# Ten heads through float32 transposes on TensorE, GpSimd copies for q and k, and new prices for the DMA queue

## The chip, the cores and the metric

One core of one Trainium2 chip runs the program. The metric is the device time of one execution in microseconds (us). Of the kernel before, three runs gave 1230.02 us (median), 1227.51 and 1231.83; a difference of about 0.3% is what such a comparison can tell from none.

Engines: PE (TensorE, matmuls; PEld is its weight load), DVE (VectorE), ACT (ScalarE), POOL (GpSimd), SP (SyncE, whose queue issues all DMA transfers here). Each engine works through its own list of instructions in order, and waits on semaphores for the others.

## The reference

Attention with a block mask over 8 batches of 8 heads (64 heads), 576 positions, 64 columns, then a mixer:

```python
scores = scale * q @ k.T                       # per head: 576 x 576
scores = where(block_i >= block_j, scores, -1e9)     # blocks of 64 positions
attn = exp(scores - max); attn = attn / (sum(attn) + 1e-9)
x = concat over heads of (attn @ v)            # 8 x 576 x 512, float32
u = x + (xt @ U @ V) transposed                # U: 576 x 32, V: 32 x 576, xt: x with positions last
out = u + relu(u @ w_ch1) @ w_ch2              # w_ch1: 512 x 2048, w_ch2: 2048 x 512
```

Everything is float32. The weights and U, V come from the host as float64 words, and the kernel turns them to float32 on the chip.

## The kernel before

**Attention.** A head's 576 query rows are cut into five tiles, i = 0 to 4 (tile 0 of 64 rows, the others of 128); tile i sees 128 i + 64 keys, so its scores are 128 x (128 i + 64). `split_qk` fetches q and k, transposed by the host, into `raw`. Heads 0 to 11 (`FS = 12`) multiply `raw` in float32 (L961). Later heads split q and k in a high and a low part (`q2`, `k1` by ACT; `q1`, `k2` by POOL, L908 and L909) and run two passes (L965, L966); for that the high part also has to lie in partitions 64 to 127, where two DMA transfers put it (L911, L912).

`softmax` puts the scores in PSUM: tile 4 in the one pair of banks `bw`, tile 3 in a bank of its own, tile 2 in another, tiles 1 and 0 in a third. DVE finds the row maximum (L979), ACT the exponential with its sum, in place in PSUM (L989). `normalise` takes the reciprocal of the sum (L1007, L1010); ACT writes the scaled probabilities as float16 (`nat`, L1022), DVE what is left of them as a second float16 (L1027), after which the bank is free. A DMA transpose (L1033) turns `nat` into `tr`, with keys in the partitions. Tiles 3 and 4 form group 1 and tiles 0 to 2 group 0, one transpose each. `split_v` cuts v into three bfloat16 pieces (POOL, L926 and L930). `apply_v` multiplies the pieces with `tr` in 33 matmuls a head (L1056); ACT and DVE join the two halves of the result (L1060, L1063) in `xt`. After two heads, `mix` transposes `xt` on PE (L1082), applies U and V (L1096, L1111) and adds (L1116).

**The mixer.** The hidden width of 2048 is worked in two halves. For the first, 16 chunks of 288 positions go through `ffn_chunk`: 96 matmuls for w1 (L477), ReLU by ACT into `hh` with the low part `hl` by DVE, 96 matmuls for w2 (L500), all of 288 columns. The first two chunks are cut in two turns. This fills PE while attention runs. The second half is done behind that by `block_products` (L671, 2688 matmuls), with fewer products by sums of blocks. Weight tiles are fetched 512 KB at a time and converted by ACT, DVE and POOL (`split64`, L327).

**What sets the order.** Nothing is issued as it is written. Each step is handed to `Plan.add` with its engine, a price in ns, a priority and the buffers that it reads and writes. `Plan.issue` (L176) plays the steps against these prices: whenever an engine is free, it takes the ready step of the lowest priority number, attention by head number, and the FFN's PE work behind all of attention (`F = 1e6 + ...`). PSUM banks are handed out there too, from lists of free ones. What comes out is one fixed list of instructions for each engine; on the chip the lists don't change. So a price moves no work by itself, it only changes the lists. Of the FFN's 3072 matmuls of the first half, these lists put 252 ahead of the end of head 16 and 2256 ahead of the end of head 63 (the last).

Of the kernel before, what the change touches and what calls it, by code (L numbers as in the profile page):

```python
# [18 lines left out]
P = 128  # L19
# [29 lines left out]
UP = 2.0 ** 15  # L49


TAIL = {"PE": 165, "DVE": 78, "ACT": 105, "POOL": 20, "SP": 0}
# [7 lines left out]
WH = 2  # L60
XB, XT, XL = 700.0, 15.6, 2500

LEAST = 2.0 ** -15
MOST = 2.0 ** 16 * (2.0 - 2.0 ** -3 - 2.0 ** -23)

QS = (0, 320, S)

TILES = ((1, 2, 0), (3, 4))
# [61 lines left out]
class Rest:  # L130
# [11 lines left out]
    def append(self, x):  # L142
        self.pool.append(x)


# [120 lines left out]
def attention_then_mixer(  # L266
# [27 lines left out]
    psp = ctx.enter_context(tc.tile_pool(name="psp", bufs=1, space=bass.MemoryType.PSUM))  # L294
    actx, pctx = ExitStack(), ExitStack()
    ap = actx.enter_context(tc.tile_pool(name="ap", bufs=1))
    hp = ctx.enter_context(tc.tile_pool(name="hp", bufs=1, side="right"))

# [134 lines left out]
    ul_r = ring(fp, KC, [P, T], F32R, "ul")  # L433
    hh_t, hl_t = (hp.tile([P, FC + 2, T], F32R, name=x) for x in ("hh", "hl"))
    hh_r, hl_r = ([Buf(t[:, n, :]) for n in range(FC + 2)] for t in (hh_t, hl_t))
    ot_t = fp.tile([P, 3, T], F32, name="ot")
    ot_r = [Buf(ot_t[:, n, :]) for n in range(3)]

    ph_t, pl_t = ([Buf(t[:, 2 * n : 2 * n + 2, :]) for n in range(FC // 2 + 1)] for t in (hh_t, hl_t))

    ffn_done = [Buf() for _ in range(NCHUNK)]

    def ffn_chunk(c, w, wb, fr=range(FC), turn=0):
# [5 lines left out]
        for k in range(KC):  # L449
            if b > 0 or turn:  # L450
                add(
                    "SP", 630, E, lambda k=k: nc.sync.dma_start(out=ur[k].ap, in_=u_d[b][:, k, o : o + T]),
                    u_s[b][k].parts, [ur[k]], after=DL,
                )
        for k in range(KC):
            uh, ul = uh_r[k], ul_r[k]
            add("ACT", _act(T, True), E, lambda u=ur[k], h=uh: nc.scalar.copy(h.ap, u.ap), [ur[k]], [uh])
            add(
                "POOL", 780, E, lambda u=ur[k], h=uh, l=ul: nc.gpsimd.tensor_sub(l.ap, u.ap, f32(h.ap)),  # L459
                [ur[k], uh], [ul],  # L460
            )
            if turn:
                add(
                    "SP", 630, E, lambda k=k: nc.sync.dma_start(out=ur[k].ap, in_=o_d[b][:, k, o : o + T]),
                    [o_s[c][k]], [ur[k]], after=DL,
                )
# [24 lines left out]
        for m in range(KC):  # L491
            ps = Buf(pool=banks)
            ms = slice(m * P, (m + 1) * P)
            ops = [(wn, f, x) for f in fr for wn, x in (("w2h", 0), ("w2l", 0), ("w2h", 1))]
            for g in range(0, len(ops), GM):

                def products(g=g, ps=ps, ms=ms, ops=ops):
                    for i in range(g, g + GM):
                        wn, f, x = ops[i]
                        nc.tensor.matmul(ps[:, :T], w()[wn][:, f, ms], hs[f][x].ap, start=(i == 0), stop=(i == len(ops) - 1))  # L500
# [9 lines left out]
            add(  # L510
                "SP", 630, E, lambda ot=ot, m=m: nc.sync.dma_start(out=o_d[b][:, m, o : o + T], in_=ot.ap), [ot],
                [o_s[c][m]], after=DL,
            )

    def block_products():
# [164 lines left out]
        for b in range(B):  # L680
# [8 lines left out]
            for t in range(CPB):  # L689
                o = t * T  # L690
                for k in range(2):
                    add(
                        "SP", 630, E,
                        lambda t=t, k=k, o=o, b=b, ur_at=ur_at: nc.sync.dma_start(
                            out=ur_at(t, k), in_=u_d[b][:, 2 * k : 2 * k + 2, o : o + T]
                        ),
                        [x for m in (2 * k, 2 * k + 1) for x in u_s[b][m].parts], [ur[t][k]], after=DL,
                    )
                for i in range(2):
                    add(  # L700
                        "SP", 630, E,
                        lambda t=t, i=i, o=o, b=b: nc.sync.dma_start(
                            out=acc_at(t, i), in_=o_d[b][:, 2 * i : 2 * i + 2, o : o + T]
                        ),
                        o_s[b * CPB + t][2 * i : 2 * i + 2], [acc[t][i]], after=DL,
                    )
# [39 lines left out]
            for stage, (parts, (w, _)) in enumerate(zip(blocks(src, STAGES2), STAGES2)):  # L746
# [8 lines left out]
                if last:  # L755

                    for i, bank in enumerate(banks):
# [8 lines left out]
                        add(  # L766
                            "SP", 630, E,
                            lambda i=i, o=b * S: nc.sync.dma_start(out=out[:, 2 + i, o : o + T], in_=acc_at(0, 1)[:, i, :]),
# [13 lines left out]
                for t, i in {3: ((0, 0),), 4: ((1, 0),), 5: ((1, 1),), 6: ((0, 1),)}.get(stage, ()):  # L782
                    o = b * S + t * T
                    add(
                        "SP", 630, E,
                        lambda t=t, i=i, o=o: nc.sync.dma_start(out=out[:, 2 * i : 2 * i + 2, o : o + T], in_=acc_at(t, i)),
# [5 lines left out]
    make_identity(nc, ident.ap)  # L792

    warm = buf(ap, [P, 1], F32, "warm")
    nc.vector.memset(warm.ap, 0.0)
# [8 lines left out]
    ss_r = [b.split(5) for b in ring(ap, 2, [P, 5], F32, "ss")]  # L804

    nat_r = [[b.split(len(TILES[g])) for b in ring(ap, 1, [P, NB[g] * P], F16, f"nat{g}")] for g in range(2)]
    tr_r = [ring(ap, 2, [P, NB[g], P], F16, f"tr{g}") for g in range(2)]
# [30 lines left out]
    for j in range(2):  # L838
        nc.vector.memset(ss_r[j].ap, 1.0)
    for g in range(2):  # L840
        for r in nat_r[g]:
            nc.vector.memset(r.ap, 0.0)

# [33 lines left out]
    def split_qk(h, pr):  # L877
# [9 lines left out]
        if h in (FS - 2, FS - 1):  # L887

            for n, (x, o) in enumerate(((q2, 0), (k2, S))):
# [3 lines left out]
                )  # L893
        add("SP", 820, pr, fetch, writes=[raw], after=DL)
        if h < FS:
# [14 lines left out]

        add("SP", 600, pr, lambda: nc.sync.dma_start(out=f32(q1[64:P]), in_=f32(q2[top])), [q2], [q1], after=DL)  # L911
        add("SP", 600, pr, lambda: nc.sync.dma_start(out=f32(k1[64:P]), in_=f32(k1[top])), [k1], [k1], after=DL)  # L912

    def split_v(h, pr):
        s = h % 2
        raw, v2 = vr_r[h // 2 % 2], v2_r[s]
        if s == 0:
            add(
                "SP", 910, pr,
                lambda: nc.sync.dma_start(out=raw[:, :, 0:64], in_=v[h // 2].rearrange("p s j d -> p (s j) d")),  # L920
                writes=raw.parts, after=DL,
            )
        mine, part = raw[:, 5 * s : 5 * s + 5, :], raw.parts[s]
        high = mine.bitcast(BF16)
# [11 lines left out]
    def softmax(h, tiles, pr):  # L936
# [48 lines left out]
        for i, at in parts:  # L985
            rows = P if i else 64

            def exponentials(i=i, at=at, rows=rows):
                nc.scalar.activation(  # L989
                    view(i, at), view(i, at), AF.Exp, bias=mx[:rows, i : i + 1], accum_out=ss[:rows, i : i + 1],  # L990
                )

            exps[i] = (bank, lambda i=i, at=at: view(i, at), Buf(), wide)
            add(
# [4 lines left out]
    def normalise(h, g, pr):  # L999
# [11 lines left out]

        add("DVE", 180, pr, inverse, [ss.parts[i] for i in tiles], [rv.parts[i] for i in tiles])
        for i in sorted(tiles, reverse=True):
# [20 lines left out]
        )  # L1034

    def apply_v(h, g, pr):
        s = h % 2
# [4 lines left out]
        me = slice(64 * s, 64 * s + 64)  # L1042
        vr, v2, tmp, tr = vr_r[h // 2 % 2], v2_r[s], take(tmp_r, "tmp"), tr_r[g][s]
        high = vr.ap.bitcast(BF16)
# [24 lines left out]
    def mix(p, pr):  # L1069
# [34 lines left out]
        for c in range(CPB):  # L1104
# [14 lines left out]
            if b == 0:  # L1119
                add(  # L1120
                    "SP", 630, pr, lambda sums=sums, dst=dst: nc.sync.dma_start(out=dst, in_=sums), [to],
                    [u_s[b][m].parts[c]], after=DL,
                )
        if b > 0:
            add(
                "SP", 820, pr, lambda: nc.sync.dma_start(out=u_d[b][:, m, :], in_=ut.ap), ut.parts, u_s[b][m].parts,
                after=DL,
# [9 lines left out]
    for h in range(NH):  # L1137
        pr = 1000.0 * h
        if h + 1 < NH:
            split_qk(h + 1, max(pr - LA, 1.0))  # L1140
        for g, tiles in ((1, (4, 3)), (0, (2, 1, 0))):
# [3 lines left out]
        for g in (1, 0):  # L1145
            apply_v(h, g, pr + 30)
        if h + 1 < NH:
# [3 lines left out]
        if h == min(WH, NH - 1):  # L1151
# [3 lines left out]
            load_w1(lambda: wa, 0, wab, lambda n: WP2 + WP3 * n, (1,), [gate])  # L1155
            load_w2(lambda: wa, 0, wab, lambda n: WP4 + WP3 * (n - FH), [gate], ks=range(FH, FC))

    for n in range(2):
# [44 lines left out]
```

## Time and profile before

| | |
|---|---|
| median of three runs | 1230.02 us |
| the profiled execution | 1232.24 us, span of its instructions 1230.5 us |
| PE busy | 1130.9 us, 92% |
| DVE, ACT, POOL busy | 998.9 us (81%), 802.0 us (65%), 324.8 us (26%) |
| mean granted clock of PE | 0.971 |
| DMA queue q1, share of 16 engines | 67.6% over the span |

Busy time of PE is that of overlapping matmuls. A row of groups reads: line, engine, operation, out<-in, shape, count, then busy us and mean ns of one, then idle time of the engine ahead of them and what ended it. A row of waits reads: who waited, for whom, us in total, times, longest. A row of the timeline reads: start and length in us, engine, line, operation, operands, count of merged instructions. A row of transfers reads: out<-in, queue, operation, count, KB each, median us from issue to landing.

### The profile page before, as it was taken

How to read it: one execution, taken by the hardware profiler on the slowest of the kernel's cores; microseconds unless marked ns; L12 is line 12 of the kernel's file. 1: busy time of each engine (PE TensorE's matmuls, PEld its weight loads, DVE VectorE, ACT ScalarE, POOL GpSimd, SP SyncE). 2: the span in 40 equal slices, each digit the busy share in tenths (PEclk: the TensorE clock that was granted, in tenths of full speed). 3: DMA queues.
4: the chain of work that ended last, by engine and by line, in shares of the span. 5: the costliest groups of instructions: out<-in, count | busy, mean ns of one | idle time of the engine just before them, and what ended most of it. 6: DMA issues, size and time to landing. Idle time of an engine off the chain costs nothing. (4 is left out here: it accounts for less than half of the span.)

```text
span 1230.5 us, 25276 instructions
## 1 busy us (share of the span) xinstructions
PE 1130.9 (92%) x9170; PEld 1067.1 (87%) x9170; DVE 998.9 (81%) x2058; ACT 802.0 (65%) x1944; POOL 324.8 (26%) x336
## 2 busy tenths in 40 slices
PE   6766895899989998998998989999999999999998
PEld 5545784888988888988898889999999999999998
DVE  7899877777787787787778875686998899889887
ACT  6777786688978778798878874343554444444543
POOL 3223454443434353353434431111000000000000
PEclk8788997999999999999999999999999999999999
DMA  8998899999999989989999994533330330330221
GB/s 152 206 211 184 195 209 195 207 200 202 192 192 185 202 185 190 193 172 217 172 211 180 188 190 94 176 112 108 97 100 27 107 116 25 92 116 31 87 78 39
DMA packets 362603, 185.62 MB, mean 151 GB/s; under 512 B 299760, under 2 KB 343792, under 8 KB 362480
## 3 DMA queue, kind: packets, MB, share of 16 engines
q1 hardware_dynamic: 362480, 184.03, 67.6%
q8 instruction: 72, 1.18, 0.4%
q14 instruction: 51, 0.42, 0.1%
HBM read 76.23 MB, written 29.49 MB: 86 GB/s over the span
## 5 line engine op out<-in xcount | busy, mean ns | idle before, releaser
L1056 PE MATMUL ba<-tr,vr 128*128 128x64 f16 (+2 forms) x1408 | 159.9, 235 | 29.5 <-DVE nat L1027 8.4
L671 PE MATMUL bb<-hh,w1l 128*128 128x288 f32 x704 | 170.1, 295 | 0.0
L671 PE MATMUL bb<-hh,w1h 128*128 128x288 f32 x704 | 169.4, 295 | 0.0
L1056 PEld LDWEIGHTS <-vr 128*128 128x128 bf16 x1408 | 103.0, 102 | 51.3 <-issue 19.7
L500 PE MATMUL bf<-hh,w2h 128*128 128x288 f32 x432 | 134.7, 312 | 1.3 <-DVE ot L506 1.3
L1027 DVE SCALAR_TENSOR_TENSOR nat<-ba,rv,nat 128x448 f16<-128x448 f32 (+3 forms) x248 | 110.0, 470 | 24.7 <-ACT nat L1022 22.5
L500 PE MATMUL bf<-hl,w2h 128*128 128x288 f32 x432 | 128.5, 297 | 0.0
L500 PE MATMUL bf<-hh,w2l 128*128 128x288 f32 x432 | 128.1, 297 | 0.0
L989 ACT ACTIVATE ba<-ba,mx 128x448 f32<-128x448 f32 (+3 forms) x248 | 108.1, 436 | 25.8 <-DVE mx L979 22.5
L671 PE MATMUL bb<-hl,w1h 128*128 128x288 f32 x576 | 123.0, 295 | 0.1
L671 PEld LDWEIGHTS bb<-hh,w1l 128*128 128x128 f32 x704 | 122.9, 190 | 0.0
L671 PEld LDWEIGHTS bb<-hh,w1h 128*128 128x128 f32 x704 | 121.9, 188 | 0.0
L1056 PE MATMUL ba<-tr,vv 128*128 128x64 f16 (+2 forms) x704 | 119.7, 234 | 0.0
L1022 ACT ACTIVATE nat<-ba,rv 128x448 f16<-128x448 f32 (+3 forms) x248 | 103.6, 462 | 14.4 <-DVE rv L1010 13.0
L625 ACT CAST hh<-hb 128x576 fp32r<-128x576 f32 x98 | 65.9, 672 | 60.6 <-PE bb L671 59.4
L908 POOL TENSOR_TENSOR q<-raw,q 64x576 fp32r<-64x576 f32 x52 | 74.6, 1435 | 93.6 <-ACT q L902 90.0
L979 DVE TENSOR_REDUCE mx<-ba 128x1 f32<-128x448 f32 (+3 forms) x248 | 92.0, 403 | 4.2 <-PE ba L966 3.2
L671 PEld LDWEIGHTS bb<-hl,w1h 128*128 128x128 f32 x576 | 91.9, 188 | 0.4 <-DVE hl L626 0.4
L477 PE MATMUL bf<-uh,w1l 128*128 128x288 f32 x456 | 90.5, 301 | 0.0
L459 POOL TENSOR_TENSOR ul<-ur,uh 128x288 fp32r<-128x288 f32 x72 | 59.7, 854 | 115.9 <-PE bg L477 68.9
L477 PE MATMUL bf<-uh,w1h 128*128 128x288 f32 x456 | 82.5, 303 | 7.6 <-DVE hl L485 6.7
L909 POOL TENSOR_TENSOR k<-raw,k 64x576 fp32r<-64x576 f32 x52 | 74.0, 1422 | 45.6 <-ACT k L907 34.5
(162 smaller groups left out, 3134.6 us busy)
## 6 DMA issues: line engine op xcount, KB each, us to landing
raw<-in_qk_dram SPq DMA_DIRECT2D x63, 288.0 KB, 4.2
st<-in_w_dram SPq DMA_DIRECT2D x32, 512.0 KB, 4.4
o_d<-ot SPq DMA_DIRECT2D x72, 144.0 KB, 2.4
vr<-in_v_dram SPq DMA_DIRECT2D x32, 320.0 KB, 4.9
ur<-u_d SPq DMA_DIRECT2D x64, 144.0 KB, 2.9
whole<-o_d SPq DMA_DIRECT2D x32, 288.0 KB, 3.1
out_dram<-whole SPq DMA_DIRECT2D x31, 288.0 KB, 2.2
ur<-u_d SPq DMA_DIRECT2D x30, 288.0 KB, 3.6
```

Of the source, the lines that this page charges most:

```text
L459: "POOL", 780, E, lambda u=ur[k], h=uh, l=ul: nc.gpsimd.tensor_sub(l.ap, u.ap, f32(h.ap)),
L477: nc.tensor.matmul(ps[:, :T], w()[wn][:, k, fs], m[k].ap, start=(i == 0), stop=(i == len(ops) - 1))
L500: nc.tensor.matmul(ps[:, :T], w()[wn][:, f, ms], hs[f][x].ap, start=(i == 0), stop=(i == len(ops) - 1))
L625: add("ACT", _act(2 * T, True), E, lambda: nc.scalar.copy(h.ap, x[0]()), [x[1]], [h])
L671: nc.tensor.matmul(bank[:, i, :T], x()[:, w(k)], p.ap[:, k, :], start=first and n == 0, stop=last and n == len(ops) - 1)
L908: add("POOL", 1380, pr, lambda: nc.gpsimd.tensor_sub(q1[top], raw[top, 0:S], f32(q2[top])), [raw, q2], [q1])
L909: add("POOL", 1380, pr, lambda: nc.gpsimd.tensor_sub(k2[top], raw[top, S : 2 * S], f32(k1[top])), [raw, k1], [k2])
L979: lambda i=i, at=at: nc.vector.tensor_reduce(out=mx[: P if i else 64, i : i + 1], in_=view(i, at), op=ALU.max, axis=AX.XY if wide else AX. ...
L989: nc.scalar.activation(view(i, at), view(i, at), AF.Exp, bias=mx[:rows, i : i + 1], accum_out=ss[:rows, i : i + 1],)
L1022: lambda x=x, hi=hi, rows=rows, i=i: nc.scalar.activation(hi, x(), AF.Copy, scale=rv[:rows, i : i + 1]),
L1027: lambda x=x, hi=hi, lo=lo, rows=rows, i=i: nc.vector.scalar_tensor_tensor(out=lo, in0=x(), scalar=rv[:rows, i : i + 1], in1=hi, op0=ALU.m ...
L1056: nc.tensor.matmul(o, w, r, start=(i == 0), stop=(i == len(ops) - 1))
```

## The change

1. **Heads 0 to 9** (`FP = 10`). The exponential goes to float32 tiles in SBUF (`pt_r`, one buffer each for tiles 0 to 3 and two for tile 4). POOL scales them in place. `transpose` turns the blocks of 128 x 128 on PE in float32 (15 a head, with `swap`, an identity whose halves are exchanged, where a half block goes to the other partitions); ACT, and DVE for one of four blocks, copy them to `pw_r`. `apply_v` is then one float32 product per key block, 8 a head of 1600 columns together, and its result is copied once. These heads have no `nat`, no DMA transpose, no `split_v`. Their tiles lie where the FFN's `hh` and `hl` come later (`hidden`), so the FFN's first ReLU comes behind head 9.
2. **Scores of later heads** take the groups (4), (3, 0) and (2, 1): two single banks and tile 4's pair.
3. **Tile 4** may take a pair of its own or, when both halves are free and more than two single banks are, the last two single banks (`Wide`).
4. **q and k**: POOL copies the high parts to partitions 64 to 127 instead of two DMA transfers a head (heads 12 to 63).
5. **Prices of the DMA queue** (SP) in the plan: 630 becomes 440, 820 becomes 560, a transpose `XB + XT * 8 * NB` goes from 2198 and 2946 ns to 1500 and 2700.

```diff
+FP = 10
+PB = (1, 1, 1, 1, 2)
-XB, XT, XL = 700.0, 15.6, 2500
+XB, XT, XL = -900.0, 25.0, 2300
+class Wide:
+    def __bool__(self):
+        return bool(self.own) or (
+            len(self.singles) > 2 and all(any(x is y for y in self.singles) for x in self.halves)
+        )
+    def pop(self, _):
+        if self.own:
+            return self.own.pop()
+        for x in self.halves:
+            del self.singles[next(n for n, y in enumerate(self.singles) if y is x)]
+        return self.pair
...
-    banks_a = [psa.tile([P, 512], F32, name=f"ba{i}") for i in range(6 - FB)]
-    banks_w = [psa.tile([P, 2, 512], F32, name="bw")]
+    pairs_a = [psa.tile([P, 2, 512], F32, name=f"ba{i}") for i in range((8 - FB) // 2)]
+    banks_a = Sorted(x[:, n, :] for x in pairs_a[:-1] for n in range(2))
+    banks_w = Wide(pairs_a[-1:], banks_a, pairs_a[-2], banks_a[-2:])
...
-        add("SP", 820, pr, fetch, writes=[raw], after=DL)
+        add("SP", 560, pr, fetch, writes=[raw], after=DL)
...
-        add("SP", 600, pr, lambda: nc.sync.dma_start(out=f32(q1[64:P]), in_=f32(q2[top])), [q2], [q1], after=DL)
-        add("SP", 600, pr, lambda: nc.sync.dma_start(out=f32(k1[64:P]), in_=f32(k1[top])), [k1], [k1], after=DL)
+        low = slice(64, P)
+        add("POOL", 740, pr, lambda: nc.gpsimd.tensor_copy(q1[low], f32(q2[top])), [q2], [q1])
+        add("POOL", 740, pr, lambda: nc.gpsimd.tensor_copy(k1[low], f32(k1[top])), [k1], [k1])
...
+        if h < FP:
+            for i in sorted(tiles, reverse=True):
+                rows, w = P if i else 64, P * i + 64
+                pt = pt_r[i][h % PB[i]]
+                x = pt[:rows, :w]
+                add(
+                    "POOL", 250 + 0.85 * w, pr,
+                    lambda x=x, rows=rows, i=i: nc.gpsimd.tensor_scalar(
+                        out=x, in0=x, scalar1=rv[:rows, i : i + 1], scalar2=1.0 / UP, op0=ALU.mult, op1=ALU.mult
+                    ),
+                    [rv.parts[i], pt], [pt],
+                )
+            return
...
+        def products():
+            for _, i, j, perm, a in moves:
+                nc.tensor.transpose(
+                    out=bank[:, a : a + P], in_=pt_r[i][h % PB[i]][:, j * P : (j + 1) * P], identity=perm.ap
+                )
+        add("PE", cost, pr, products, pts, [bank], hold=[b])
+        copy((g, part) == (0, 1), n, pr, lambda: pw[:, span], lambda: bank[:, :n], [bank], [b])
...
+            def whole_products():
+                for j in range(NK[g]):
+                    a = max(P * j - q0, 0)
+                    nc.tensor.matmul(
+                        bank[:, a:n], vr[:, 5 * s + j, :], pt[:, _at(g, j)], start=(j == 0), stop=(j == NK[g] - 1)
+                    )
...
-            for x in ((4,), (3,)) if g else ((2,), (1, 0)):
-                softmax(h, x, pr + 10)
+        groups = (((4,), (3,)), ((2,), (1, 0))) if h < FP else (((4,), (3, 0)), ((2, 1),))
...
+    early = [b for x in pw_r for y in x for b in y.parts] + [b for x in pt_r for b in x]
+    add("SP", 0, -1.0, hidden, early, hh_r + hl_r, hold=early)
```

**The order on PE, first heads.** Before, the beginning of the product with v for group 0 of head 1 (`tr`: transposed float16 probabilities; `vr`, `vv`: pieces of v):

```order
L1056 LDWEIGHTS vr0_152
L1056 MATMUL ba1_96<-tr01_145,vr0_152 128x256
L1056 LDWEIGHTS vr0_152
L1056 MATMUL ba1_96<-tr01_145,vr0_152 128x64
L1056 LDWEIGHTS vr0_152
L1056 MATMUL ba1_96<-tr01_145,vr0_152 128x256
```

Now, the same group of head 0: transposes of `p0` to `p2`, with the other group's products and the other head's scores between them, then three float32 products (`pw`: transposed probabilities):

```order
L1161 MATMUL ba0_95<-ident_113,p0_0_141 128x128
L1161 MATMUL ba0_95<-ident_113,p1_0_142 128x128
L1161 MATMUL ba0_95<-ident_113,p2_0_143 128x128
L1187 MATMUL ba1_96<-pw0_1_148,vr0_161 128x256 x3
L1187 MATMUL ba1_96<-pw0_1_148,vr0_161 128x192
L1187 MATMUL ba1_96<-pw0_1_148,vr0_161 128x64
L1161 MATMUL ba0_95<-swap_118,p1_0_142 128x128
L1161 MATMUL ba0_95<-swap_118,p2_0_143 128x128
L1161 MATMUL ba0_95<-ident_113,p2_0_143 128x128
L1037 MATMUL bf0_90<-raw0_137 128x448
```

33 matmuls of a head have become 15 transposes and 8 products; no transfer stands between them.

**The order on SP, end of attention.** `tr` is a DMA transpose, `o_d5` or `o_d4` the stored FFN result of batch 5 or 4, and `u_d` its input. Before:

```order
L911 DMA q1_1_149<-q2_1_135 64x576
L912 DMA k1_1_151<-k1_1_151 64x576
L1033 DMA_TRANSPOSE tr10_146<-nat10_143 128x18x128
L1033 DMA_TRANSPOSE tr00_144<-nat00_142 128x12x128
L1033 DMA_TRANSPOSE tr11_147<-nat10_143 128x18x128
L1126 DMA u_d7_81<-ut0_169 128x576
L1033 DMA_TRANSPOSE tr01_145<-nat00_142 128x12x128
L511 DMA o_d5_87<-ot_116 128x288
```

Now:

```order
L1131 DMA_TRANSPOSE tr00_153<-nat00_151 128x12x128
L1131 DMA_TRANSPOSE tr11_156<-nat10_152 128x18x128
L570 DMA o_d4_86<-ot_112 128x288
L511 DMA ur0_102<-u_d5_79 128x288
L1278 DMA u_d7_81<-ut0_178 128x576
L1131 DMA_TRANSPOSE tr01_154<-nat00_151 128x12x128
L570 DMA o_d4_86<-ot_112 128x288
```

The copies of q and k are gone, and when the last head is transposed the FFN is in batch 4 and no longer in batch 5. Counted on PE, 12 FFN matmuls stand ahead of the end of head 9 (30 before), 288 ahead of that of head 16 (252), 1698 ahead of that of head 63 (2256).

**Tile 4 and POOL.** In the new lists all 64 heads have tile 4 in the pair `ba2`, which is its own (before: `bw`). Two heads in a row on PE, before and now:

```order
L965 MATMUL bw_99<-k1_0_150,q1_0_148 128x288
...
L965 MATMUL bw_99<-k1_1_151,q1_1_149 128x288
```

```order
L1041 MATMUL ba2_97<-k1_0_159,q1_0_157 128x288
...
L1041 MATMUL ba2_97<-k1_1_160,q1_1_158 128x288
```

The list of the last two single banks is never drawn on for tile 4.

On POOL the copies (CAST) stand behind both subtractions of their head:

```order
L981 TENSOR_TENSOR q1_1_158<-raw1_138,q2_1_134 64x576
L982 TENSOR_TENSOR k2_1_136<-raw1_138,k1_1_160 64x576
L985 CAST q1_1_158<-q2_1_134 64x576
L986 CAST k1_1_160<-k1_1_160 64x576
L1006 TENSOR_TENSOR vv0_163<-vr0_161 128x5x64
```

More of the change, by code (lines that the diff above doesn't have):

```diff
@@ L792, in attention_then_mixer @@
     make_identity(nc, ident.ap)
+    swap = buf(ap, [P, P], F32, "swap")
+    for a in (0, 64):
+        nc.vector.tensor_copy(swap[:, a : a + 64], ident[:, 64 - a : P - a])
     warm = buf(ap, [P, 1], F32, "warm")
@@ L1034, in normalise, with copy, transpose @@
         )
+    def copy(vector, n, pr, out, inp, reads, writes):
+        if vector:
+            add("DVE", _dve(n), pr, lambda: nc.vector.tensor_copy(out(), inp()), reads, writes)
+        else:
+            add("ACT", _act(n), pr, lambda: nc.scalar.copy(out(), inp()), reads, writes)
+    def transpose(h, g, part, pr):
+        js = BLOCKS[g][part]
+        bank, span = Buf(pool=banks_a), _span(g, js)
+        n = span.stop - span.start
+        moves = []
+        for j in js:
+            for i in range(5):
+                q0 = max(P * i - 64, 0)
+                a, b = max(q0, _first(g, j)), min(P * i + 64, QS[g + 1])
+                if a < b:
+                    c = _at(g, j).start - span.start + a - _first(g, j)
+                    half = b - a < P
+                    left = half and c + P > 512
+                    moves.append((not half, i, j, swap if half and i and not left else ident, c - 64 if left else c))
+        moves.sort(key=lambda m: m[0])
+        def products():
[3 more added lines that the diff above has]
+                )
+        cost = 109 * len(moves)
+        pts = [pt_r[i][h % PB[i]] for i in sorted({m[1] for m in moves})]
+        pw = pw_r[h % 2][g]
+        b = pw.parts[part]
+        add("PE", cost, pr, products, pts, [bank], hold=[b])
+        copy((g, part) == (0, 1), n, pr, lambda: pw[:, span], lambda: bank[:, :n], [bank], [b])
     def apply_v(h, g, pr):
```

108 lines of the change are left out of this document (86 added, 22 removed).

## The prediction

> **What bounds the kernel now.** I read the windows view first, over stretches cut at the ends of heads 9, 16 and 63, then one dense stretch and the stretch 300 to 700. After each length stand, by engine, busy time and (instructions), then TensorE's granted clock, the DMA engines' share, GB/s.
>
> ```profile
> 0.00:125.20 125.20, 88.56 (x575) 66.20 (x576) 106.29 (x263) 91.65 (x246) 40.90 (x53) 0.85 0.90 189
> 125.20:221.80 96.60, 74.51 (x600) 67.01 (x600) 77.11 (x175) 71.78 (x193) 43.87 (x43) 0.86 0.96 201
> 221.80:760.10 538.30, 500.77 (x4479) 467.32 (x4479) 414.08 (x1019) 430.88 (x1172) 227.87 (x229) 0.99 0.93 189
> 760.10:1230.50 470.40, 467.06 (x3521) 466.57 (x3520) 401.37 (x602) 207.71 (x334) 12.20 (x12) 1.00 0.29 87
> 300.00:700.00 400.00, 371.34 (x3325) 345.44 (x3326) 312.61 (x765) 328.02 (x892) 173.83 (x174) 0.99 0.95 193
> 1050.00:1100.00 50.00, 50.00 (x379) 50.00 (x378) 44.02 (x65) 23.82 (x38) 0.00 (x0) 1.00 0.32 96
> ```
>
> Call the first two stretches together A (heads 0 to 16), the third B (heads 17 to 63), the fourth C (mixer alone). The dense stretch issues 379 matmuls of 288 columns in 50 us: 0.132 us each, 0.458 ns a column. Busy time hides how far TensorE is from that pace, since matmuls overlap, so I count work at its pace. The timeline gives the other prices and the cuts:
>
> ```profile
> L671 PE MATMUL bb<-hh,w1h 128*128 128x288 f32 x704 | 169.4, 295 | 0.0
> 6.55 0.92 PE L961 MATMUL bf<-raw 128*128 128x448 f32 x2
> 61.02 0.60 PE L1082 MATMUL ba<-ident,xt 128*128 128x128 f32 x4
> 124.97 0.19 PE L1056 MATMUL ba<-tr,vv 128*128 128x64 f16 x1
> 221.62 0.19 PE L1056 MATMUL ba<-tr,vv 128*128 128x64 f16 x1
> 759.93 0.19 PE L1056 MATMUL ba<-tr,vv 128*128 128x64 f16 x1
> ```
>
> A matmul lasts 295 ns and the next starts after 132, so a group ends in a tail of 0.163 us. One float32 product of 448 columns is recorded as two passes in 0.92: (0.92-0.163)/896 = 0.845 ns a column and pass, 1.69 a column. Four float32 transposes take 0.60: (0.60-0.163)/4 = 0.109 us each.
>
> A head has 1600 columns of scores (192+320+448+576+64) and 4800 columns of probability times v in 33 matmuls (2.20 us). Its share of the mix is half of 5 transposes, 9 products of 128 columns and 2 of 288: 0.67. Heads 0 to 11 score in float32, 2.70; the others in two passes of 0.458, 1.47. So 5.57 and 4.34 us a head. Of the FFN's 3072 matmuls in the first half, 252 stand ahead of head 16's end and 2256 ahead of head 63's; 816 and block_products' 2688 follow.
>
> A: 12x5.57+5x4.34+252x0.132 = 122 us of work in 221.8. B: 47x4.34+2004x0.132 = 468 in 538.3. C: 3504x0.132 = 462 in 470.4. TensorE loses 100, 70 and 8 us; it bounds C outright, and the time is its work plus what it loses in A and B.
>
> In A VectorE is at 106.29 of 125.20, 0.85, and tile 4's one PSUM pair waits for it:
>
> ```profile
> PEld bw L961 <- DVE nat L1027: 13.6, 6, 4.2
> PE bw L961 <- DVE nat L1027: 12.4, 5, 4.1
> ```
>
> In B the DMA engines stand at 0.93 to 0.95, more than any engine's rate of work.
>
> **The change part by part.** *Heads 0 to 9, TensorE.* 33 matmuls (2.20) become 15 transposes (15x0.109 = 1.64) and 1600 float32 columns (2.70): +2.14 us a head, +21 in all. Nothing hides this in the sum; it must be earned from what A loses.
>
> *The same heads, the other engines.* These rows price what goes and what comes:
>
> ```profile
> L1027 DVE SCALAR_TENSOR_TENSOR nat<-ba,rv,nat 128x448 f16<-128x448 f32 (+3 forms) x248 | 110.0, 470 | 24.7 <-ACT nat L1022 22.5
> L1022 ACT ACTIVATE nat<-ba,rv 128x448 f16<-128x448 f32 (+3 forms) x248 | 103.6, 462 | 14.4 <-DVE rv L1010 13.0
> L1063 DVE SCALAR_TENSOR_TENSOR xt<-ba,tmp 64x256 f32<-64x256 f32 (+1 forms) x128 | 57.0, 446 | 17.6 <-ACT tmp L1060 15.2
> L1060 ACT ACTIVATE tmp<-ba 64x256 f32<-64x256 f32 (+1 forms) x128 | 52.0, 407 | 24.0 <-PE ba L1056 21.4
> L1027 DVE SCALAR_TENSOR_TENSOR nat<-bw,rv,nat 128x576 f16<-128x576 f32 x64 | 52.3, 816 | 29.3 <-ACT nat L1022 28.6
> L1022 ACT ACTIVATE nat<-bw,rv 128x576 f16<-128x576 f32 x64 | 47.3, 740 | 16.8 <-ACT ba L989 5.8 <-issue 4.9 <-DVE rv L1010 3.3
> L1085 ACT CAST xh<-ba 128x512 fp32r<-128x512 f32 x32 | 18.6, 582 | 9.5 <-PE ba L1082 9.3
> L908 POOL TENSOR_TENSOR q<-raw,q 64x576 fp32r<-64x576 f32 x52 | 74.6, 1435 | 93.6 <-ACT q L902 90.0 <-PE bf L500 3.6
> L828 POOL MEMSET raw<- 64x1152 f32 x2 | 2.1, 1055 | 0.1
> L926 POOL TENSOR_TENSOR vr<-vr 128x320 f32<-128x320 f32 x64 | 45.9, 730 | 114.9 <-DMA vr<-in_v_dram 107.3 <-PE bw L966 7.7
> ```
>
> VectorE loses (110.0+52.3+57.0)/64 = 3.43 us a head and gains one copy of 256 columns, about 0.41: 106.3-30 = 76 for ten heads. ScalarE loses (103.6+47.3+52.0)/64 = 3.17, and gains copies of 512, 512 and 320 columns (0.58 for 512, about 0.4 for 320 by L1060's row) and two of the output (2x0.41): 2.4; 91.65-8 = 84. GpSimd scales 1600 columns a head in place. No row shows one tensor in and out on GpSimd; bounds are the memset, 1055/1152 = 0.92 ns a column, and the two-input subtraction, 1435/576 = 2.49: 1.5 to 4.0 us. I take the middle, 1.7: 2.7 us. It drops two subtractions of v (2x0.73). At 41+13 of 100 us GpSimd is not the bound; even at 4.0 it is 66. TensorE's 10x7.71+2 = 79 stands close behind ScalarE. With ScalarE at the 0.85 that VectorE reaches here, these heads take 84/0.85 = 99: I take 100 instead of 125. The pair is then released by the exponential, not by the low half's product, which removes the two waits on bw. Bounds: 92 (ScalarE at 0.91) and 125 (no gain).
>
> *Heads 10 to 16* keep the old path. The FFN's hidden tiles now lie where heads 0 to 9 keep their probabilities, so its first ReLU waits for head 9: 12 FFN matmuls stand ahead of that head's end instead of 30, and what waits is the FFN alone. Heads 10 to 16 then carry 276: 2x5.57+5x4.34+276x0.132 = 69 us of work, at B's 0.87 (468/538.3) 80; with the last weight tiles among them I take 82 (bounds 78, 85). A becomes 182 (170 to 210).
>
> *Tile 4's two banks.* The order puts every tile 4 into the same pair as before, so the choice is never used: 0.
>
> *Copies of q and k.* Removed from B are two transfers a head:
>
> ```profile
> q<-q SPq DMA_DIRECT2D x52, 144.0 KB, 3.3
> k<-k SPq DMA_DIRECT2D x52, 144.0 KB, 3.3
> o_d<-ot SPq DMA_DIRECT2D x72, 144.0 KB, 2.4
> tr<-nat SPq DMA_TRANSPOSE x128, 4.6
> ```
>
> B spends 0.93x538.3/47 = 10.65 us of DMA time a head, and moves 189 GB/s x 538.3/47 = 2165 KB. The copies are 288 KB, 13% or 1.4 us; the transposes, which stay, move in short packets and cost more by the byte, so I take 1.1. On GpSimd each copy lies between 576x0.92 = 0.53 and 1.43 us, mid 0.98: 2.0 a head on 227.87/47 = 4.85. GpSimd at 6.9 has room, but the copies stand behind both subtractions in its queue, so scores may wait about 2 us longer than for a transfer; they are prepared a head ahead, which covers it.
>
> *The order.* The new queue prices take no time themselves; with them, and with two single banks of scores a head beside the pair instead of three, the planner sets heads closer: 1698 FFN matmuls stand ahead of head 63's end, not 2256. B holds 1410, 30 a head instead of 42.6, and C 1374+2688 = 4062. C is then 4062x0.132+8 = 544 us, nearly certain. B's work is 47x4.34+1410x0.132 = 390; its time is the head's pace, bounded thrice. PE: 8.30 us of work at 0.87 is 9.5. DMA: 10.65-1.1, less the FFN transfers that go (12.6/192 of a chunk's eight of 144 KB, 76 KB, 0.35 us) is 9.2 with no pause, 9.9 at 0.93. ScalarE: 430.88/47 = 9.17, some 8.9 with fewer FFN casts, 9.8 at 0.91. I take 10.0: 470 us (432 at 9.2; 538 at the old 11.45).
>
> *The sum.* 182+470+544 = 1196 in the span; the profiled execution was 1232.24 for a span of 1230.5, +1.7, and 2.2 above the median 1230.02: **1196** on the median's scale.
>
> **The rivals.** (1) *Denser still.* Heads 0 to 9 in 95 and B at 9.3: 177+437+544 = 1158. For it: DMA is relieved and waits on bw go. Against: three engines near 0.9 at once. 15%. (2) *Early gain alone.* B at 10.4, as short packets keep the DMA full: 182+489+544 = 1215. 15%. (3) *Heads 0 to 9 no faster.* The ring of probabilities has one buffer for tiles 0 to 3, so exponentials wait on GpSimd's scaling and the transposes; at 2.49 ns a column the loop could keep 12.5 us a head: 207+470+544 = 1221. 13%. (4) *Slower: the pace of heads doesn't follow the order.* The FFN matmuls have been moved behind head 63; if B still needs 11.45 us a head, TensorE idles where they were: 182+538+544 = 1264. It decides from 504/47 = 10.7 on. For it: the DMA share, and transposes that stay. Against: 11% of the DMA's load goes, and 0.35 us more. 12%. (5) *Slower: the clock.* In heads 0 to 9 of before, with (10x5.57+30x0.132)/125.2 = 48% of TensorE's pace used, the clock fell:
>
> ```profile
> 30.00:45.00 15.00, 12.78 (x84) 9.23 (x82) 10.82 (x28) 11.22 (x29) 1.98 (x2) 0.78 0.93 227
> 60.00:75.00 15.00, 8.41 (x67) 6.02 (x65) 13.65 (x36) 11.36 (x32) 3.48 (x5) 0.96 0.97 215
> 105.00:120.00 15.00, 9.91 (x79) 7.50 (x79) 14.53 (x35) 11.05 (x31) 5.59 (x6) 1.00 0.87 188
> ```
>
> If transposes didn't count as work for it, 7.71 us would be 15.4 at half clock: 154+5+82+470+544 = 1255; it decides below a clock of about 0.57. Against: used pace rises to near 0.8, and the four transposes quoted ran at 0.109 us, as long as a full-speed pass over 128 columns by the float32 row (128x0.845 = 108). 5%. The Trainium skill ("TensorE: Matmul & The Clock Gate", Part 4: PE-mode transpose) says just that: the full clock doesn't engage for transposes, as they don't count as busy. No stretch here holds enough transposes to test it; by that rule the result is this rival's.
>
> **How the numbers follow.** The forecast has 40% (its own range 1182 to 1212), the rivals 15, 15, 13, 12 and 5. The range cuts 8% off the low end (A 172, B at 9.4: 1158, less a little) and 12% off the high one: 1154 to 1232. What can be told from no change here is 0.3%, 1226 to 1234. Faster: the forecast, (1), most of (2) and (3): 0.81. Same 0.05. Slower 0.14.
>
> **What would show it.** Head 9's last product ends near 100, head 16's near 182, head 63's near 652. In the first 100 us ScalarE is busiest, no wait on the wide pair remains, and the clock is above 0.9. In B the DMA share stays above 0.9 at 30 FFN matmuls a head, and C runs at 0.132 a matmul. A pace of 10.7 or more, or a clock near half in the first heads, makes the forecast wrong; a scaling row above 2.5 ns a column would show GpSimd's price missed.

## The result and the profile after

The changed kernel takes 1358.26 us (median, 1356.76 to 1359.56) beside 1230.55 for the kernel before: 1.104 times as long, 95% interval 1.1017 to 1.1066. It is slower by 128 us where 34 us less was forecast.

The windows view of the changed kernel is cut as in the prediction, at the ends of heads 9, 16 and 63. Columns: stretch, length, busy us and (instructions) of PE, PEld, DVE, ACT and POOL, TensorE's granted clock, DMA share, GB/s.

```profile
0.00:131.10 131.10, 104.86 (x540) 80.89 (x540) 78.28 (x216) 87.50 (x236) 61.80 (x90) 0.95 0.43 112
131.10:232.40 101.30, 78.77 (x654) 70.85 (x653) 79.30 (x177) 74.31 (x195) 55.79 (x60) 0.97 0.87 183
232.40:813.10 580.70, 449.40 (x3880) 407.46 (x3881) 396.51 (x975) 424.81 (x1124) 271.30 (x302) 0.96 0.70 143
813.10:1357.80 544.70, 541.09 (x4078) 540.60 (x4077) 417.89 (x638) 221.86 (x370) 21.23 (x24) 1.00 0.27 81
```

The four stages are 5.9, 4.7, 42.4 and 74.3 us longer than before. The last is as forecast (544 forecast, 544.7 measured). The surprise is the third. It holds 594 FFN matmuls fewer, some 78 us less of work, and is longer. None of its shares is high: DVE 396.51 of 580.70 is 0.68, ACT 0.73, the DMA engines 0.70 (0.93 before), and TensorE's pace uses 390 of 580.7. When every engine idles for a quarter of the time or more, no engine is the bound: they wait for one another. The view of waits in that stage (who <- for whom: us, times, longest) names where:

```profile
ACT ba L1075 <- DVE mx L1055: 31.2, 45, 2.2
PE ba L1041 <- DVE nat L1125: 25.4, 29, 2.5
DVE mx L1055 <- ACT ba L1075: 12.1, 14, 1.8
PE ba L1208 <- ACT ba L1075: 9.9, 8, 1.9
ACT nat L1120 <- DVE nat L1125: 9.4, 18, 1.9
```

L1041 writes scores into a bank, L1055 takes their maximum, L1075 the exponential, L1120 and L1125 read it out, and L1208 multiplies with v. In the changed kernel `ba` is the name of tile 4's pair too, which was `bw` before, so the rows above compare with the sums of both names. Before, in heads 17 to 63:

```profile
ACT bw L989 <- DVE mx L979: 18.4, 17, 3.3
ACT ba L989 <- DVE mx L979: 13.9, 23, 2.6
PE ba L965 <- DVE nat L1027: 6.0, 11, 1.4
PE ba L1056 <- ACT ba L989: 1.0, 1, 1.0
```

The first pair cost as much before (32.3 us against 31.2). The second and the fourth have grown, from 6.0 to 25.4 and from 1.0 to 9.9. The third and the fifth have no row there, and the third looks impossible: a maximum (L1055) is the first reader of fresh scores, and the exponential of a tile needs its maximum. A maximum can wait for an exponential only if that is another tile's, in the same bank or in another one. In the changed kernel each single bank is a half of a tile of two banks.

### The profile page after: what moved, and what is told of

It reads as the page before. It is cut to its first block, busy times and chain, and to the rows that moved or that the text cites. A ratio compares the mean times of both kernels' runs of the same rounds, so it can differ in the third digit from the quotient of the medians.

```text
span 1357.8 us, 25198 instructions
## 1 busy us (share of the span) xinstructions
PE 1174.1 (86%) x9150; PEld 1099.8 (81%) x9150; DVE 972.0 (72%) x2005; ACT 808.5 (60%) x1924; POOL 410.1 (30%) x474
## 5 line engine op out<-in xcount | busy, mean ns | idle before, releaser
L1125 DVE SCALAR_TENSOR_TENSOR nat<-ba,rv,nat 128x576 f16<-128x576 f32 x270 | 141.8, 544 | 70.4 <-ACT nat L1120 36.6
L1055 DVE TENSOR_REDUCE mx<-ba 128x1 f32<-128x320 f32 (+3 forms) x312 | 139.2, 474 | 61.3 <-ACT ba L1075 13.8
L1075 ACT ACTIVATE ba<-ba,mx 128x576 f32<-128x576 f32 (+1 forms) x270 | 133.6, 495 | 62.9 <-DVE mx L1055 36.2
L1208 PE MATMUL ba<-tr,vr 128*128 128x64 f16 (+2 forms) x1188 | 128.4, 229 | 47.8 <-ACT ba L1075 10.7
L1120 ACT ACTIVATE nat<-ba,rv 128x576 f16<-128x576 f32 x270 | 131.0, 522 | 44.4 <-DVE rv L1095 14.4
L1041 PE MATMUL ba<-k,q 128*128 128x288 f32 (+4 forms) x312 | 97.7, 331 | 50.5 <-DVE nat L1125 29.7
L1208 PEld LDWEIGHTS <-vr 128*128 128x128 bf16 x1188 | 85.6, 99 | 63.4 <-issue 44.7
L559 PE MATMUL bf<-hh,w2h 128*128 128x288 f32 x368 | 117.4, 319 | 0.7 <-DVE hl L544 0.7
L1041 PEld LDWEIGHTS ba<-k,q 128*128 128x128 f32 (+1 forms) x312 | 58.3, 187 | 63.1 <-DVE nat L1125 25.1
L1208 PE MATMUL ba<-tr,vv 128*128 128x64 f16 (+2 forms) x594 | 98.2, 229 | 0.0
```

The lines of the kernel that those rows point to most:

```text
L1041: nc.tensor.matmul(o, q1[:, qs], k1[:, ks], start=True, stop=False)
L1055: lambda i=i, at=at: nc.vector.tensor_reduce(out=mx[: P if i else 64, i : i + 1], in_=view(i, at), op=ALU.max, axis=AX.XY if wide else AX. ...
L1075: nc.scalar.activation(out, view(i, at), AF.Exp, bias=mx[:rows, i : i + 1], accum_out=ss[:rows, i : i + 1],)
L1120: lambda x=x, hi=hi, rows=rows, i=i: nc.scalar.activation(hi, x(), AF.Copy, scale=rv[:rows, i : i + 1]),
L1125: lambda x=x, hi=hi, lo=lo, rows=rows, i=i: nc.vector.scalar_tensor_tensor(out=lo, in0=x(), scalar=rv[:rows, i : i + 1], in1=hi, op0=ALU.m ...
L1208: nc.tensor.matmul(o, w, r, start=(i == 0), stop=(i == len(ops) - 1))
```

## The experiments

**First: one part alone, or all but one.** Theories at this point: the shared score groups, the moved FFN matmuls, the queue's new times, the copies. Three kernels are the one before with one part of the change added, the fourth is the changed one with one part taken back.

```diff
 b_groups (before with the new groups)
-            for x in ((4,), (3,)) if g else ((2,), (1, 0)):
+            for x in ((4,), (3, 0)) if g else ((2, 1),):
 b_prices (before with the queue's new times)
-XB, XT, XL = 700.0, 15.6, 2500
+XB, XT, XL = -900.0, 25.0, 2300
-    "SP", 630 ...   "SP", 820 ...
+    "SP", 440 ...   "SP", 560 ...
 b_pool (before with the copies on GpSimd)
-        add("SP", 600, pr, lambda: nc.sync.dma_start(out=f32(q1[64:P]), ...
+        add("POOL", 740, pr, lambda: nc.gpsimd.tensor_copy(q1[low], f32(q2[top])), [q2], [q1])
 a_groups (changed kernel with the old groups)
-        groups = (((4,), (3,)), ((2,), (1, 0))) if h < FP else (((4,), (3, 0)), ((2, 1),))
+        groups = (((4,), (3,)), ((2,), (1, 0)))
```

> The kernel before with one part of the change: scores of all heads in the groups (4), (3, 0) and (2, 1). Three theories. Sharing: two tiles in one bank make TensorE, VectorE and ScalarE wait for each other in stage B, and that is most of the 128 us; then this one is slower by 60 to 130 us and stage B takes 12 us a head or more. Moved work: the pace of heads stays at 11.45 us whatever the list says, and each FFN matmul that the list moves behind head 63 costs 0.132 us; 1992 instead of 2256 stand ahead of its end, so +35 us, 1265. Forecast (pace follows the list): 1230 or a little less.

> The kernel before with one part of the change: the new prices of the DMA queue in the plan, so that only the lists differ. Sharing: no change of more than 10 us. Moved work: 2106 FFN matmuls ahead of head 63's end instead of 2256, 150 x 0.132 = +20 us, 1250. Prices: if transposes that are planned too early stall TensorE, +40 us and more, with waits of the v products on the transposes.

> The kernel before with one part of the change: GpSimd copies the high parts of q and k. Copies: if scores wait for the copies behind both subtractions, +40 us and more and waits of TensorE on GpSimd. Moved work: 2094 instead of 2256 matmuls, +21 us, 1251. Forecast: DMA relief shortens stage B by about 10%, 1210 or less.

> The changed kernel with four groups of scores for all heads, as before: (4), (3), (2), (1, 0). Sharing: most of the loss comes back, 1250 or less, and TensorE's waits of scores on VectorE's low halves fall from 25 us to about 6. Moved work: 2046 FFN matmuls ahead of head 63's end instead of 1698, 348 x 0.132 = 46 us back, 1312. Heads 0 to 9 are as in the changed kernel, 131 us.

Measured, one time each, beside 1228.06 for the kernel before: groups 1237.05 (+9.0), queue's times 1230.39 (+2.3), copies 1223.04 (-5.0). The changed kernel with the old groups took 1347.09, 11 less than with the new. Forecasts missed here: the groups alone were to take 1230 or a little less, the copies 1210 or less, and neither time named for the old groups (1250, 1312) came. Added up, the parts tried alone give +6 us, not +128. The theory that the groups are the loss falls, and with it every theory that puts the loss in one of these parts alone. Left were the float32 transposes and a part that had been priced at nothing: the allocation of the banks.

**Second: the banks alone.** `a_sep` is the changed kernel with a tile for each single bank; `b_pair` is the kernel before with its single banks as halves of two tiles. Instruction for instruction, the five engines' lists equal those of their parents except for the banks' names and what is waited for. In `b_pair` every instruction also addresses the same physical bank as in the kernel before.

```diff
 a_sep
-    pairs_a = [psa.tile([P, 2, 512], F32, name=f"ba{i}") for i in range((8 - FB) // 2)]
-    banks_a = Sorted(x[:, n, :] for x in pairs_a[:-1] for n in range(2))
+    pairs_a = [psa.tile([P, 2, 512], F32, name="bw")]
+    banks_a = Sorted(psa.tile([P, 512], F32, name=f"ba{i}") for i in range(6 - FB))
-    banks_w = Wide(pairs_a[-1:], banks_a, pairs_a[-2], banks_a[-2:])
+    banks_w = Wide(pairs_a, banks_a, None, ())
 b_pair
-    banks_a = [psa.tile([P, 512], F32, name=f"ba{i}") for i in range(6 - FB)]
+    pairs_a = [psa.tile([P, 2, 512], F32, name=f"ba{i}") for i in range((6 - FB) // 2)]
+    banks_a = [x[:, n, :] for x in pairs_a for n in range(2)]
```

> The changed kernel with its four single banks as four tiles of one bank each, and the wide bank as a tile of its own, as before the change; tile 4 has that one pair alone. All five engines' lists are those of the changed kernel, but for the names of banks. Theory Halves: the two banks that are halves of one pair tile wait for each other's writers and readers although no instruction touches both, so every hand-over between PE, DVE and ACT on a single bank comes late. The waits on tiles called ba in the heads 17 to 63 then fall: the 580.7 us of that stage go to 470 to 530, and the time to 1190 to 1300. Rival List: the loss comes from the new list of work (fewer FFN matmuls between the heads' parts); the tiles change nothing, and the time stays at 1345 to 1360. Rival Transposes: the loss is in the ten float32 heads and what they delay; it too stays at 1345 to 1360.

> The kernel before with one change: its four single banks are the halves of two pair tiles; its lists stay as they were. Theory Halves: the stage of heads 17 to 63 gets longer though no instruction and no order differs: time beyond the pace of the matmuls there rises from 76 us towards the 197 us of the changed kernel, and the time from 1228 to 1280 to 1370. Rivals List and Transposes: 1225 to 1235, no change.

Measured: `a_sep` 1222.02 us, ratio to the kernel before 0.994 (0.9914 to 0.9966). `b_pair` 1355.31, ratio 1.1031 (1.0995 to 1.1066). The allocation alone makes the kernel before as slow as the changed one, and without it the changed one is a little faster than before. Windows of `b_pair`, then of `a_sep`, same cuts:

```profile
0.00:142.00 142.00, 96.65 (x575) 70.06 (x576) 105.99 (x263) 93.63 (x246) 40.48 (x53) 0.78 0.76 168
142.00:251.30 109.30, 77.38 (x600) 68.31 (x600) 77.43 (x175) 73.12 (x192) 43.74 (x43) 0.83 0.81 177
251.30:882.50 631.20, 519.62 (x4480) 476.54 (x4479) 413.95 (x1019) 441.91 (x1173) 228.55 (x229) 0.98 0.76 161
882.50:1352.80 470.30, 466.96 (x3520) 466.47 (x3519) 401.56 (x602) 207.74 (x334) 12.21 (x12) 1.00 0.28 87
```

```profile
0.00:105.10 105.10, 94.37 (x540) 75.89 (x540) 84.35 (x216) 85.79 (x236) 63.32 (x89) 1.00 0.51 137
105.10:192.00 86.90, 76.22 (x654) 68.80 (x653) 78.23 (x175) 72.36 (x193) 56.43 (x59) 0.98 0.97 212
192.00:674.30 482.30, 426.30 (x3881) 390.92 (x3881) 389.96 (x978) 413.88 (x1127) 272.12 (x302) 0.99 0.87 173
674.30:1218.90 544.60, 541.12 (x4079) 540.64 (x4078) 417.67 (x638) 222.18 (x370) 21.05 (x24) 1.00 0.26 81
```

By stage the pair tiles cost the kernel before 16.8, 12.7, 92.9 and 0 us, and the changed kernel 26.0, 14.4, 98.4 and 0. DVE's busy time hardly moves (413.95 and 414.08 us in the third stage of `b_pair` and of before), so what grew is waiting. The last stage, without heads, works in the same banks through tiles of its own (`bg`, `bb`) and doesn't change.

How it costs time is seen in one head of `b_pair`. Rows of its timeline (start, length, engine, line, operation, tiles; in brackets the idle time before it and who ended it), in order of time:

```profile
659.90 0.61 DVE L979 TENSOR_REDUCE mx<-ba 128x1 f32<-128x448 f32 x1
660.56 0.41 PE L965 MATMUL ba<-k,q 128*128 128x320 f32 x1 [1.29 <-DVE mx L979]
660.81 0.31 PE L966 MATMUL ba<-k,q 128*128 128x320 f32 x1
661.16 0.61 ACT L989 ACTIVATE ba<-ba,mx 128x448 f32<-128x448 f32 x1 [1.10 <-PE ba L966]
661.91 0.76 DVE L979 TENSOR_REDUCE mx<-ba 128x1 f32<-128x320 f32 x2 [1.05 <-ACT ba L989]
662.72 0.38 PE L1056 MATMUL ba<-tr,vr 128*128 128x256 f16 x2 [0.44 <-DVE mx L979]
```

The 448 columns of tile 3 lie in one bank and the 320 of tile 2 in another; no value passes between them here. Yet TensorE may not write the 320 before VectorE has read the 448; ScalarE may not take the exponential of the 448 before TensorE has written the 320; and VectorE may not read the 320 before that exponential is done. Three engines that should work side by side take turns, and TensorE stands behind them. All three waits are in the program of `b_pair`, and none is in that of the kernel before. VectorE's lists at this place, with the engine that each row waits for (`ba2`, `ba3` are single banks; in `b_pair`, `ba1` is the pair, and the two maxima read different halves of it), before and in `b_pair`:

```
1106 L979 TENSOR_REDUCE mx0_156<-ba2_97 128x1 [waits PE_49]
1107 L506 TENSOR_TENSOR ot_116<-bf1_91,ur1_105 128x288 [waits DMAHW2_49,PE_49]
1108 L979 TENSOR_REDUCE mx0_156<-ba3_98 128x1 [waits PE_49]
```

```
1104 L979 TENSOR_REDUCE mx0_154<-ba1_96 128x1 [waits PE_49]
1105 L506 TENSOR_TENSOR ot_114<-bf1_91,ur1_103 128x288 [waits DMAHW2_49,PE_49]
1106 L979 TENSOR_REDUCE mx0_154<-ba1_96 128x1 [waits Activation_49]
```

Of the 320 maxima none waits for ScalarE in the kernel before, and 28 do in `b_pair`; in the changed kernel 39 do, in `a_sep` 3. In the programs all 28 wait for ScalarE's work on the other half of their pair (17 times an exponential), and so do 37 of the 39 (20 times an exponential); the 3 of `a_sep` wait for work on their own tile. Waits of L1027 for TensorE rise from 0 to 40, and those of L965 for ScalarE from 12 to 39. So the waits are made when the program is built: accesses to one tile are ordered even where they touch different halves. It is no conflict of the banks, since `b_pair` uses the same ones in the same order as the kernel before. The Trainium skill ("PSUM — Partial Sum Buffer", "PSUM bank collisions raise a hardware error") keeps engines apart only where they touch the same bank; nothing there asks for waits between two banks, and `a_sep`, without them, is 136 us faster. With separate tiles, these rows are left of the five in heads 17 to 63:

```profile
PE ba L1041 <- DVE nat L1125: 14.3, 22, 1.3
ACT bw L1075 <- DVE mx L1055: 9.6, 12, 1.6
PE bw L1041 <- DVE nat L1125: 6.7, 12, 0.9
ACT ba L1075 <- DVE mx L1055: 4.8, 8, 2.0
ACT nat L1120 <- DVE nat L1125: 1.3, 5, 0.5
```

The waits for an exponential (the third and fourth row of the changed kernel, 12.1 and 9.9 us) are gone, and the fifth falls from 9.4 to 1.3. With tile 4's pair counted in both, scores wait for the read-out nearly as long as in the changed kernel (21.0 us against 25.4), so that row is no mark of the pair tiles.

**Third: the pair tiles with other parts taken back.** If the float32 heads, or the copies, were behind the waits, the loss would go with them.

```diff
 a_fp0
-FP = 10
+FP = 0
 a_dma
-        add("POOL", 740, pr, lambda: nc.gpsimd.tensor_copy(q1[low], f32(q2[top])), [q2], [q1])
+        add("SP", 440, pr, lambda: nc.sync.dma_start(out=f32(q1[64:P]), in_=f32(q2[top])), ...
```

> The changed kernel with FP = 0: no head is transposed by PE in float32, all 64 go through float16 and DMA transposes as before the change. Theory Halves: the loss stays, 1320 to 1370 us, since it is made in heads 17 to 63, which have the same path in both. Rival Transposes: the time returns below 1290 us.

> The changed kernel with the high parts of q and k copied by DMA again and not by GpSimd. Theory Halves: 1340 to 1380 us, since the copies are on no path that the banks set. Rival: the copies hold up GpSimd, whose results the scores of tile 4 wait for; the time then falls below 1320 us.

Measured once each: `a_fp0` 1387.61, `a_dma` 1361.79 us. The loss stays; `a_fp0` is even above the range named. Both rivals fall.

**Fourth: the parts over separate tiles.** The same edits on `a_sep`; `s_pg` has the old groups and the queue's old times, so that the float32 heads and the copies are what is left of the change.

> The changed kernel with separate bank tiles, and the old four groups (4), (3), (2), (1, 0) in the heads from 10 on. 2046 FFN matmuls are listed ahead of the end of the last head, where the list of separate tiles alone has 1698. Theory Sharing: 348 fewer matmuls behind the heads take 46 us off the last stage (0.132 us each), and the heads 10 to 63, with a group more each, get 30 to 40 us longer: 1205 to 1217, since the kernel before lost 9 us by the other way. Rival: the shared groups save nothing, and the whole 46 us shows: below 1200. Rival: they save more than the matmuls cost: above 1224.

> The changed kernel with separate bank tiles and FP = 0: the first ten heads transpose through float16 and DMA again. The forecast's step: heads 0 to 9 then end near 125 us and not near 105, the last stage has 54 matmuls fewer (7 us): 1230 to 1242. Rival: PE's 21 us more of work for the transposes cost as much as the wait that they take away: 1215 to 1225, no difference.

> The changed kernel with separate bank tiles, and the high parts of q and k brought by DMA again. Copies on GpSimd are worth 5 us alone in the kernel before; if they are worth the same here: 1224 to 1232, with a list that has 72 matmuls fewer at the end (9 us). Rival: nothing, 1215 to 1223.

> The changed kernel with separate bank tiles, the old four groups and the old times of SP's queue: what is left of the change is the float32 transposes and the copies on GpSimd. 2136 matmuls are listed ahead of the last head's end. If the parts add up as they did alone (groups -9, copies -5, transposes -10 to -20 against before): 1200 to 1212, the fastest so far. Rival: more work among the heads makes them as much longer, 1215 to 1228.

| lists of | pair tiles | separate tiles | difference | against before, separate (interval) |
|---|---|---|---|---|
| the kernel before | 1355.31 | 1230.26 | 125 | 1 |
| the change | 1358.26 | 1222.02 | 136 | 0.994 (0.9914-0.9966) |
| old groups (`a_groups`, `s_groups`) | 1347.09 | 1210.34 | 137 | 0.9846 (0.9818-0.9874) |
| no float32 heads (`a_fp0`, `s_fp0`) | 1387.61 | 1240.91 | 147 | 1.0091 (1.0061-1.0121) |
| q, k by DMA (`a_dma`, `s_dma`) | 1361.79 | 1235.94 | 126 | 1.005 (1.0029-1.007) |
| old groups and queue times (`s_pg`) | | 1195.66 | | 0.9724 (0.9701-0.9747) |

Five pairs of lists lose 125 to 147 us to the tiles (the last three of the five ran once with pair tiles). `s_groups` and `s_fp0` came within their forecasts; `s_dma` came 4 us above its range and `s_pg` 4 us below. From 1222, taking back the float32 heads costs 19 us and the copies 14; taking back the groups gains 12, and the queue's times 15 more. What the float32 heads are worth shows in the first stage, 127.2 us in `s_fp0` and 105.1 in `a_sep`:

```profile
0.00:127.20 127.20, 84.46 (x565) 63.01 (x566) 109.68 (x277) 96.74 (x257) 47.82 (x59) 0.89 0.89 192
```

The copies were worth 5 us in the kernel before (one run) and are worth 14 here. The windows of `s_dma` suggest why:

```profile
105.90:198.90 93.00, 76.60 (x659) 70.26 (x659) 81.81 (x181) 73.72 (x196) 48.17 (x47) 0.96 1.04 219
198.90:699.80 500.90, 439.25 (x3949) 403.79 (x3949) 399.81 (x977) 413.41 (x1127) 210.66 (x210) 0.98 0.95 194
```

Its DMA share is 1.04 and 0.95 where `a_sep` has 0.97 and 0.87: with the transfers back, the DMA engines fill these stages. That is a reading of two rows, not an experiment of its own.

`s_pg` beats both kernels: 1195.66 us, 2.8% faster than before. Its windows:

```profile
0.00:102.30 102.30, 93.34 (x536) 74.14 (x537) 84.14 (x214) 82.92 (x229) 64.19 (x89) 1.00 0.52 141
102.30:191.30 89.00, 79.51 (x666) 71.35 (x666) 79.77 (x179) 73.67 (x195) 57.34 (x58) 0.96 0.97 207
191.30:706.90 515.60, 482.66 (x4314) 446.38 (x4313) 402.67 (x1004) 422.30 (x1158) 279.93 (x312) 0.99 0.83 168
706.90:1193.70 486.80, 482.92 (x3642) 482.43 (x3640) 405.05 (x611) 211.66 (x344) 14.95 (x16) 1.00 0.27 85
```

Its list has 2136 FFN matmuls ahead of head 63's end, not 1698. These 438 take 57.8 us out of the last stage (544.6 to 486.8), which is 0.132 each, and put 33.3 into heads 17 to 63 (482.3 to 515.6), where TensorE had gaps for the rest.

## Why the prediction was wrong

One step failed, the shortest: "*Tile 4's two banks.* The order puts every tile 4 into the same pair as before, so the choice is never used: 0." The first half holds, the choice is never used. The conclusion doesn't: to offer the choice, the four single banks became halves of two tiles, and that acts on every score, every read-out and every product of the heads, used or not. I priced the use of the choice and not the form of the buffers that makes it possible. The diff shows that form in the line of `banks_a`; the five points of the change name only the choice. Measured, this step is +139 us of the span (1357.8 against 1218.9), and no rival named it.

The other steps, with the tiles apart (`a_sep`) so that they can be seen:

| stage | forecast | changed kernel | with separate tiles |
|---|---|---|---|
| heads 0 to 9 | 100 | 131.1 | 105.1 |
| heads 10 to 16 | 82 | 101.3 | 86.9 |
| heads 17 to 63 | 470 | 580.7 | 482.3 |
| last stage | 544 | 544.7 | 544.6 |
| span | 1196 | 1357.8 | 1218.9 |

- **Heads 0 to 9.** The reasoning holds: head 9 ends at 127.2 us in `s_fp0` and at 105.1 in `a_sep`, a gain of 22 (25 forecast), though these heads of `s_fp0` also take the new score groups. TensorE's waits for VectorE on tile 4's pair (12.4 us) are gone. ScalarE's 84 us came as 85.79, and ScalarE ran at 0.82 of the stage, not 0.85. VectorE's 76 came as 84.35. The same 216 instructions took it 78.28 in the changed kernel; what grew most is the conversion of weights (L408: 716 ns in the changed kernel, 850 in `a_sep`), and no run says why.
- **Prices of GpSimd.** Copies and scaling in the changed kernel's groups (busy us, mean ns of one):

```profile
L985 POOL CAST q<-q 64x576 fp32r<-64x576 f32 x52 | 34.3, 660 | 3.1
L1105 POOL TENSOR_SCALAR p<-p,rv 128x576 f32<-128x576 f32 (+4 forms) x50 | 29.8, 609 | 40.7 <-DVE rv L1095 26.1 <-ACT raw L971 9.3 <-DVE z L416 2.6
```

  The scaling is 29.8/10 = 3.0 us a head (2.7 forecast), 1.86 ns a column; a copy takes 0.66 (0.98 forecast, inside its bounds). Rival 3, GpSimd's scaling as a bound at 2.49 ns a column, falls.
- **Copies.** The DMA time per head in heads 17 to 63 is 0.95x500.9/47 = 10.1 us in `s_dma` and 0.87x482.3/47 = 8.9 in `a_sep`: 1.2 less, 1.1 forecast. The share itself was to stay above 0.9 there, and is 0.87, so the DMA engines weren't full.
- **The order.** The last stage is exact. Heads 17 to 63 need 10.26 us each in `a_sep`, 10.0 forecast, so rival 4 (the pace doesn't follow the order) falls too: its mark, 10.7, was passed in the changed kernel (12.36), but through the tiles. In `s_pg`, with 438 more FFN matmuls ahead of the last head's end, it is 515.6/47 = 10.97. The new groups and queue times, which move these matmuls behind the heads, are still a loss, 26 us between `a_sep` and `s_pg`; the forecast had netted it against the faster heads without asking which list is better.
- **The clock.** Rival 5 falls: 0.95 in the changed kernel's first stage, 1.00 in `a_sep`'s.

So mechanism and sizes of the other steps held within 23 us: 5, 5 and 12 us over in the first three stages. With the tiles apart the time, 1222, lies in the range but above the forecast's own 1182 to 1212. Rival 3's 1221 is near it by luck alone, since heads 0 to 9 did get faster; rival 2 comes nearest in its mechanism, with 10.4 us a head in heads 17 to 63, but the full DMA that it gave as the reason isn't there (0.87). What sets the 23 us is open. In heads 17 to 63 of `a_sep` DMA stands at 0.87 and ScalarE at 413.88/482.3 = 0.86, neither full, and no run separates them.

## What to carry to other kernels

Price a change of how a buffer is allocated as a change of every instruction that touches it: two buffers in one tile can be ordered against each other by the program, though the lists of work are equal. In a trace the mark is a stage that gets longer while all engines' shares fall, and waits between instructions that exchange no data (a first reader that waits for a later step). Compare what the same instruction waits for in the two lists before trusting that "not used" means "costs nothing".

## What the runs showed of the hardware

In the first ten heads the granted clock was lower where less of TensorE's pace was used. By the prediction's prices their work is an estimated 60 us before and 79 with the float32 heads. That is 0.42 of the 142.0 us of `b_pair`, with a clock of 0.78; 0.48 of the 125.2 us of the kernel before, with 0.85; 0.60 of the 131.1 us of the changed kernel, with 0.95; and 0.75 of the 105.1 us of `a_sep`, with 1.00. Busy time in the prediction's three stretches of 15 us doesn't follow this (12.78 us with 0.78, 8.41 with 0.96), so it is a tendency over whole stages and not a rule.

The float32 transposes kept the pace that the prediction had read; one row of the changed kernel's timeline:

```profile
60.51 0.60 PE L1161 MATMUL ba<-ident,p 128*128 128x128 f32 x4
```

Four take 0.60 us, as before the change. The Trainium skill ("TensorE: Matmul & The Clock Gate", Part 4: PE-mode transpose) says that the full clock doesn't engage for transposes, which don't count as busy in the same way. Here 150 of them, some 16 of the 79 us, left it at 1.00 among products in `a_sep`. A stretch of transposes alone was not run, so that rule is not tested here.
